# Block 3's state projection in a mixed S5 and SwiGLU layer: the shared term is added by accumulating DMAs instead of VectorE

## The chip, the cores and the metric

The kernel runs on one core of one Trainium2 chip. The metric is the device time of one execution in microseconds (us), the median over runs. Lines (L792) are those of the kernel before, and engines go by the names of the profile: PE is TensorE's matmul, PEld its weight load, DVE is VectorE, ACT is ScalarE, POOL is GpSimd, SP is SyncE.

## The reference

For one sequence of 2048 tokens with 512 features, the layer norm of x feeds two branches, and their sum is added to x. One is a diagonal state-space recurrence with 512 complex states, the other a SwiGLU of width 1792. All inputs and the output are bf16.

```python
xn = layernorm(x)
# branch A: state space
Lam_bar = exp(dt * Lam)                         # 512 complex numbers
Bu = einsum("bld,pd->blp", xn, B_bar)           # the state projection
h[t] = Lam_bar * h[t - 1] + Bu[t]
yA = 2 * real(einsum("blp,dp->bld", h, C)) + xn * Dskip
# branch B: SwiGLU
yB = (silu(xn @ w1) * (xn @ w3)) @ w2
return x + yA + yB
```

## The kernel before

**Blocks and pairs.** The tokens are cut into 4 blocks of 512 (`b` = 0 to 3), each of 4 chunks of 128. For each block there is a layer norm, the state projection, the recurrence, and the gates of the SwiGLU. Both branches' outputs are one product at the end: the tile `act` holds, for every chunk, gates and states in fp16, and it is multiplied by w2 and C together. This is done for two chunks at a time, which the code calls a pair: `pairs[n]` is block n // 2, chunks 2 (n % 2) and the next, n = 0 to 7.

**Seven products instead of eight.** The output of a pair (`y_fast`) is a 2 by 2 block product that is done with seven block products by sums and differences of the operands (Strassen's scheme in Winograd's form). `row_sums` makes the sums of the `act` side, and `product1` to `product7` are the seven, 11 matmuls each, in an order such as 1, 4, 2, 6, 5, 7, 3. One sum, s4, overwrites the operand a12 as soon as product 2 has used it. In pairs 2 to 5 this is an accumulating DMA from GpSimd's queue (L1093), and product 3 reads it as its weights. In pairs 4 and 5 product 3 is put off into the next pair (`LATER`).

**The state projection of blocks 2 and 3** (`bu_fast(b, hf)`, for each half `hf` of the states) uses the same scheme: products `one` to `seven`, four matmuls each. Of the PSUM tiles, `e` gets product five, and ScalarE copies it to SBUF as `s5`, the shared term, in f32. Two quarters of the result u are the finished PSUM tile evicted by ScalarE (`copy`). The other two are a PSUM tile plus `s5`, and VectorE adds and evicts them (`add`, L792) as bf16. In block 3 these steps are spread over the output products of pairs 2 (first half of the states) and 3 (second half), one step after each of their first five products:

```python
        return deque(((one, five), (two, six), (seven,), (three,), (four,)))
```

**The recurrence** (`ssm_tasks`) takes u through pre_a (L484) and pre_b (L488), two multiplications by a table of cosines and sines; pre_c, which adds the two, on VectorE or as an accumulating DMA (L495); four scans (L505); post_a and post_b (L513, L519), which turn back and write the states into `act`; and post_c, the sum of these two, for block 2 as an accumulating DMA (L527). In block 3 these tasks lie behind block 2's.

**What sets the order.** The order of the instructions on each engine is that of the program, which a planner (`Filler`, `bg`) writes. It keeps a queue of VectorE's background tasks (steps of the recurrence, sums, tables) with an estimated cost for each, and two clocks: `pe`, which `bg.tensor(us)` advances for each product, and `dve`, which every task and every `bg.own(us)` (VectorE work that is tied to a product) advances. `bg.fill()` emits tasks from the queue's head while they fit under `pe` plus a lead of 1.7 us:

```python
    def own(self, us, after=0.1):
        self.dve = max(self.dve, self.pe + after) + us
...
        limit = self.pe + (self.lead if lead is None else lead)
        while self.tasks and self.dve + 0.5 * self.tasks[0][0] <= limit:
```

A task that is a DMA costs 0. GpSimd's queue takes its DMAs in the order of the program, and each waits there for its own inputs.

**After pair 3** come the gates of block 3 (`glu_last`, L848, L869, L879), where VectorE does block 3's pre-steps in between, and then pairs 4 to 7.

Of the kernel before, what the change touches and what calls it, by code (L numbers as in the profile page):

```python
# [11 lines left out]
ALU = mybir.AluOpType  # L12
ACT = mybir.ActivationFunctionType

FP32 = DT.float32
BF16 = DT.bfloat16
FP16 = DT.float16
P = 128
# [45 lines left out]
def kernel(  # L64
# [17 lines left out]
    nc = tc.nc  # L82
# [4 lines left out]
    TBLK = CPB * P  # L87
# [29 lines left out]
    glup = ctx.enter_context(tc.tile_pool(name="glup", bufs=3))  # L117
# [29 lines left out]
    tabe = const.tile([P, NPT, 3, TBLK], BF16, name="tabe")  # L147
# [163 lines left out]
    gp = nc.gpsimd  # L311
# [28 lines left out]
    def sin_step(until=None):  # L340
        while sins and (until is None or until not in sins_done):
            key, fn = sins.popleft()
            fn()
            sins_done.add(key)
            if until is None:
                break
# [73 lines left out]
    def k_state(pt, ri=0):  # L420
        return (NFH if pt < NPH else NK + NFH - 2 * NPH) + 2 * pt + ri
# [13 lines left out]
    def act_state(b, hf):  # L435
        k = k_state(2 * hf)
        return act(b)[:, :, k:k + 4, :]

    def by_state(v):
        return v.rearrange("p c (j r) t -> p j r c t", r=2)  # L440

    u_blk = {}
# [19 lines left out]
    def ssm_tasks(b, posts_last=False, between=(), middle=(), late=()):  # L462
        FULL = [P, 2, 2, TBLK]

        def by_chunk(v):
            return v.rearrange("p j r (c t) -> p j r c t", t=P)

        def half(hf):
            psl = slice(2 * hf, 2 * hf + 2)
            st = {}  # L470

            def pre_a():
                if b == 0:
                    sin_step((2 * hf + 1, 1))
                    nc.vector.tensor_scalar(out=tabe[:, psl, 2, :], in0=tabe[:, psl, 1, :], scalar1=-1.0,
                                            scalar2=None, op0=ALU.mult)
                st["g"] = u_blk[b, hf]
                if (b, hf) == (3, 0):
                    st["p"] = up.tile(FULL, BF16, name="u")
                elif b == NBLK - 1:  # L480
                    st["p"] = xtp.tile([P, NDT, TBLK], BF16, name="xnT").rearrange("p (j r) t -> p j r t", r=2)
                else:
                    st["p"] = ssmw.tile(FULL, BF16, name="p")
                nc.vector.tensor_tensor(out=st["p"][:, :, ::-1, :], in0=st["g"], in1=tabe[:, psl, 2:0:-1, :],  # L484
                                        op=ALU.mult)

            def pre_b():
                nc.vector.tensor_tensor(out=st["g"], in0=st["g"], in1=tabe[:, psl, 0:1, :].to_broadcast(FULL),  # L488
                                        op=ALU.mult)

            def pre_c():
                if b == 0 or (b, hf) == (2, 0):
                    nc.vector.tensor_tensor(out=st["g"], in0=st["g"], in1=st["p"], op=ALU.add)
                else:
                    gp.dma_start(out=st["g"], in_=st["p"], accum_op=ALU.add)  # L495

            def scan(j, ri):
                pt = 2 * hf + j
                init = 0.0
                if b in (1, 2):  # L500
                    init = ends[:, hf, 2 * j + ri:2 * j + ri + 1]
                elif b > 2:
                    init = act_blk[b - 1][:, CPB - 1, k_state(pt, ri), P - 1:P]
                v = st["g"][:, j, ri, :]
                nc.vector.tensor_tensor_scan(out=v, data0=rho[:, pt:pt + 1].to_broadcast([P, TBLK]), data1=v,  # L505
                                             initial=init, op0=ALU.mult, op1=ALU.add)

            def post_a(csl=slice(0, CPB)):
                if "p16" not in st:
                    st["p16"] = ssmw.tile(FULL, BF16, name="p").bitcast(FP16).rearrange(  # L510
                        "p j r (c t) -> p (j r c t)", t=P).rearrange("p (c k t) -> p c k t", c=CPB, t=P)
                tsl = slice(csl.start * P, csl.stop * P)
                nc.vector.tensor_tensor(out=by_state(st["p16"][:, csl]), in0=by_chunk(st["g"][:, :, ::-1, tsl]),  # L513
                                        in1=by_chunk(tabe[:, psl, 2:0:-1, tsl]), op=ALU.mult)

            def post_b(csl=slice(0, CPB)):
                tsl = slice(csl.start * P, csl.stop * P)
                n = csl.stop - csl.start
                nc.vector.tensor_tensor(out=by_state(act_state(b, hf)[:, csl]), in0=by_chunk(st["g"][:, :, :, tsl]),  # L519
                                        in1=by_chunk(tabe[:, psl, 0:1, tsl]).to_broadcast([P, 2, 2, n, P]), op=ALU.mult)  # L520

            def post_c(csl=slice(0, CPB)):
                a, p16 = act_state(b, hf)[:, csl], st["p16"][:, csl]
                if b == NBLK - 1 and (hf == 1 or csl.start > 0):
                    nc.vector.tensor_tensor(out=a, in0=a, in1=p16, op=ALU.add)
                else:
                    gp.dma_start(out=a, in_=p16, accum_op=ALU.add)  # L527

            if (b, hf) == (1, 1):
                pre_c.ready = lambda: ("squares", 2, CPB - 1) in sins_done  # L530
            pre_a.ready = lambda: (b, hf) in u_blk
            scans = [lambda j=j, ri=ri: scan(j, ri) for j in range(2) for ri in range(2)]
            return (pre_a, pre_b, pre_c), scans, (post_a, post_b, post_c)

        (pre0, scans0, post0), (pre1, scans1, post1) = (half(hf) for hf in range(NPT // 2))

        transfers = (post0[2],) + (() if b == NBLK - 1 else (post1[2],)) + ((pre1[2],) if b > 0 else ()) + ((pre0[2],) if b in (1, 3) else ())

        def add(*fns):
            for fn in fns:  # L540
                bg.add(0.0 if fn in transfers else 1.2 if fn in scans0 or fn in scans1 else 1.16, fn,
                       ("scan", b) if fn in scans0 else ("post", b) if fn in post0 else ("ssm", b))

        if b == 0:
            add(*pre0, *scans0, *post0, *pre1, *scans1, *post1)
            return
        add(*pre0)
        for t in middle:
            bg.add(*t)
        if b != 2:  # L550
            add(*pre1)
        for t in between:
            bg.add(*t)
        if b == 2:
            for t in late:
                bg.add(*t)
            add(*pre1)
        add(*scans0)
        if b != 2:
            for t in late:  # L560
                bg.add(*t)
        if posts_last:
            add(*scans1)
            return lambda: add(*post0, *post1)
        if b < NBLK - 1:
            add(*post0, *scans1, *post1)
            return

        def by_tokens(fns, h):
            part = slice(h * CPB // 2, (h + 1) * CPB // 2)  # L570
            return [(0.0 if fn is post0[2] and h == 0 else 0.6, lambda fn=fn: fn(part), ("ssm", b)) for fn in fns]

        for t in by_tokens(post0, 0):
            bg.add(*t)
        add(*scans1)
        for t in by_tokens(post1, 0):
            bg.add(*t)
        return by_tokens(post0, 1) + by_tokens(post1, 1)
# [163 lines left out]
    def bu_columns(b):  # L742
        if b == 3:
            return ups["t"]
        return act(2)[:, :, k_gate(10):k_gate(10) + 4, :].rearrange("p c (k a) t -> p c k (a t)", k=2)
# [14 lines left out]
    def bu_fast(b, hf):  # L760
        a11, a12, a22 = bu_quarter(hf, 0, 0), bu_quarter(hf, 1, 0), bu_quarter(hf, 1, 1)
        s1, s2, s3, s4 = bu_rows(hf)
        t = bu_columns(b)
        t1, t2, t3, t4 = (t[i] if b == 3 else t[:, i] for i in range(4))
        b11, b12, b21, b22 = quarters(b)
        if (b, hf) == (3, 1):
            u = x_blk[3].rearrange("p (j r) t -> p j r t", r=2)
        else:
            u = up.tile([P, 2, 2, TBLK], BF16, name="u")
        s5 = glup.tile([P, 2, TBLK], BF16, name="g16").bitcast(FP32).rearrange("p a t -> p (a t)")  # L770
        if (b, hf) != (3, 1):
            f, z = (ps_bu.tile([P, TBLK], FP32, name="bu_ps") for _ in range(2))
            e, g = (ps_y.tile([P, TBLK], FP32, name="y_ps") for _ in range(2))
        else:
            f, z, e, g = (ps_gu.tile([P, TBLK], FP32, name="gu_ps") for _ in range(4))
# [8 lines left out]
        def copy(out, x):  # L784
            nc.scalar.activation(out=out, in_=x, func=ACT.Copy)

        def parts(ps):
            return ps.rearrange("p (h t) -> p h t", h=2)

        def add(out, ps):  # L790
            bg.own(0.7)
            nc.vector.tensor_tensor(out=out, in0=parts(ps), in1=parts(s5), op=ALU.add)  # L792

# [21 lines left out]
        def three():  # L815
            product(e, s4, b22)
            add(u[:, 0, :, TH:TBLK], e)
# [465 lines left out]
```

## Time and profile before

| what | value |
|---|---|
| time, median of 3 runs (lowest to highest) | 201.09 us (201.04 to 201.39) |
| span of the profiled execution, first to last instruction | 199.5 us |
| median less that span | 1.59 us |
| mean granted TensorE clock | 0.999 |
| TensorE busy | 195.6 us (98%) |
| VectorE busy | 181.8 us (91%) |
| ScalarE busy | 135.0 us (68%) |
| GpSimd busy | 51.5 us (26%) |
| L792 on VectorE, PSUM plus shared term, 128x512 | 8 of them, 0.66 to 0.69 us; 4 in block 3 |
| L785 on ScalarE, PSUM to SBUF, 128x512 to bf16 | 8 of them, 0.59 to 0.61 us |
| L1093, the DMA that makes s4, 352 KB | 3.8 us from issue to landing |
| L527, the DMA that adds the two post products, 512 KB | 5.4 to 9.1 us for the whole blocks, 4.3 us for half a block |

The profile is of one execution. Its time is the span, and what the metric adds around it is taken to be the 1.59 us between the span and the median. Busy shares are averages over stages with different limits. The chain of waits, followed back from the last instruction, tells what set the end. A landing is counted from the start of the instruction that issues the DMA.

### The profile page before, as it was taken

How to read it: one execution, taken by the hardware profiler on the slowest of the kernel's cores; microseconds unless marked ns; L12 is line 12 of the kernel's file. 1: busy time of each engine (PE TensorE's matmuls, PEld its weight loads, DVE VectorE, ACT ScalarE, POOL GpSimd, SP SyncE). 2: the span in 40 equal slices, each digit the busy share in tenths (PEclk: the TensorE clock that was granted, in tenths of full speed). 3: DMA queues.
4: the chain of work that ended last, by engine and by line, in shares of the span. 5: the costliest groups of instructions: out<-in, count | busy, mean ns of one | idle time of the engine just before them, and what ended most of it. 6: DMA issues, size and time to landing. Idle time of an engine off the chain costs nothing.

```text
span 199.5 us, 3700 instructions
## 1 busy us (share of the span) xinstructions
PE 195.6 (98%) x1401; PEld 130.7 (65%) x1401; DVE 181.8 (91%) x254; ACT 135.0 (68%) x281; POOL 51.5 (26%) x75
## 2 busy tenths in 40 slices
PE   8999999999999999999999999999999999999994
PEld 2774444444444488866555468888566678888893
DVE  3689699999999999989999997999999999999972
ACT  4699897699999996968998684362588783111220
POOL 7180289700411134041202305040021303310000
PEclk9999999999999999999999999999999999999999
DMA  4999996991497054730997455838137732941111
GB/s 138 326 277 200 302 186 124 343 273 23 69 181 141 0 105 82 135 105 0 156 148 119 89 92 98 172 83 132 53 59 129 149 56 52 174 92 36 53 44 40
DMA packets 32258, 25.12 MB, mean 126 GB/s; under 512 B 16240, under 2 KB 29936, under 8 KB 32240
## 3 DMA queue, kind: packets, MB, share of 16 engines
q0 software_dynamic: 6128, 11.38, 33.5%
q1 hardware_dynamic: 25536, 13.21, 26.8%
q10 hardware_dynamic: 576, 0.30, 0.5%
q8 instruction: 11, 0.18, 0.4%
q14 instruction: 7, 0.06, 0.1%
HBM read 7.74 MB, written 2.10 MB: 49 GB/s over the span
## 4 chain that ended last, share of the span: by engine, by line
PE 95%; DMA 2%; SPq 1%; issue 0%; DVE 0%
PE gu_ps L587 34%; PE gu_ps L1054 17%; PE y_ps L1054 10%; PE gu_ps L848 7%; PE bu_ps L1054 7%; PE bu_ps L454 3%; PE y_ps L454 3%; PE y_ps L869 3%; PE y_ps L780 3%; DMA w_sb<-in_B_w_dram 2%; PE gu_ps L619 2%; PE gu_ps L780 2%; PE bu_ps L869 1%; PE bu_ps L780 1%; PE bu_ps L619 1%; SPq L166 0%
## 5 line engine op out<-in xcount | busy, mean ns | idle before, releaser
L587 PE MATMUL gu_ps<-xnT,w_sb 128*128 128x512 bf16 x312 | 69.6, 379 | 0.0
L587 PEld LDWEIGHTS <-w_sb 128*128 128x128 bf16 x312 | 30.5, 98 | 34.2
L1054 PEld LDWEIGHTS <-act 128*128 128x128 f16 x462 | 43.5, 98 | 5.4
L596 ACT ACTIVATE g<-gu_ps 128x512 bf16<-128x512 f32 x41 | 24.8, 606 | 6.0 <-PE gu_ps L587 3.6
L597 ACT ACTIVATE u<-gu_ps 128x512 bf16<-128x512 f32 x41 | 24.8, 606 | 4.5 <-PE gu_ps L587 3.7
L505 DVE TENSOR_TENSOR_SCAN u<-rho,ends,u 128x512 bf16<-128x512 f32 x16 | 20.0, 1270 | 0.0
L527 POOL DMA_DIRECT2D act<-p x7 | 9.2, 1320 | 34.0 <-DVE act L519 22.1
L1054 PE MATMUL gu_ps<-w_sb,act 128*128 128x256 bf16 (+3 forms) x126 | 16.0, 267 | 0.0
L848 PE MATMUL gu_ps<-xnT,w_sb 128*128 128x512 bf16 x64 | 15.9, 379 | 0.0
L604 DVE TENSOR_TENSOR act<-g,u 128x1024 f16<-128x1024 bf16 x21 | 14.2, 679 | 0.4 <-ACT u L597 0.4
L860 ACT ACTIVATE g<-gu_ps 128x512 bf16<-128x512 f32 x14 | 8.4, 599 | 5.4 <-PE gu_ps L848 5.0
L454 PEld LDWEIGHTS <-bt 128*128 128x128 bf16 x64 | 6.3, 98 | 7.5
L1077 ACT ACTIVATE x_blk<-gu_ps 128x256 f32<-128x256 f32 (+1 forms) x9 | 3.3, 368 | 10.6 <-PE gu_ps L1054 10.6
L1054 PE MATMUL bu_ps<-w_sb,act 128*128 128x256 bf16 (+3 forms) x84 | 10.4, 264 | 0.0
L1054 PE MATMUL gu_ps<-ct,act 128*128 128x256 f16 (+1 forms) x72 | 10.4, 267 | 0.0
L848 PEld LDWEIGHTS <-w_sb 128*128 128x128 bf16 x64 | 6.3, 98 | 4.8
L505 DVE TENSOR_TENSOR_SCAN u<-rho,u 128x512 bf16<-128x512 f32 x8 | 9.2, 1206 | 0.0
L1054 PEld LDWEIGHTS <-x_blk 128*128 128x128 f16 x88 | 8.6, 98 | 1.0
L1054 PEld LDWEIGHTS <-tw 128*128 128x128 f16 x88 | 8.6, 98 | 1.0
L513 DVE TENSOR_TENSOR p<-u,tabe 128x2048 f16<-128x2048 bf16 (+1 forms) x8 | 8.7, 1085 | 0.1
L519 DVE TENSOR_TENSOR act<-u,tabe 128x2048 f16<-128x2048 bf16 (+1 forms) x8 | 8.7, 1083 | 0.0
L488 DVE TENSOR_TENSOR u<-u,tabe 128x2048 bf16<-128x2048 bf16 x7 | 8.5, 1219 | 0.1
(203 smaller groups left out, 392.5 us busy)
## 6 DMA issues: line engine op xcount, KB each, us to landing
act<-p POOLq DMA_DIRECT2D x6, 512.0 KB, 6.1
xn<-x_blk POOLq DMA_DIRECT2D x4, 512.0 KB, 5.5
out_dram<-xn SPq DMA_DIRECT2D x15, 128.0 KB, 1.7
w_sb<-in_B_w_dram SPq DMA_DIRECT2D x1, 1792.0 KB, 8.2
act<-act POOLq DMA_DIRECT2D x5, 352.0 KB, 4.6
w_sb<-in_B_w_dram SPq DMA_DIRECT2D x2, 768.0 KB, 6.4
u<-p POOLq DMA_DIRECT2D x3, 512.0 KB, 5.1
w_sb<-in_B_w_dram SPq DMA_DIRECT2D x4, 256.0 KB, 4.9
```

Of the source, the lines that this page charges most:

```text
L454: nc.tensor.matmul(out=ps, lhsT=bt[:, ri, dt, pt * P:(pt + 1) * P], rhs=xnT_blk[b][:, dt, :], start=(dt == 0), stop=(dt == NDT - 1))
L505: nc.vector.tensor_tensor_scan(out=v, data0=rho[:, pt:pt + 1].to_broadcast([P, TBLK]), data1=v, initial=init, op0=ALU.mult, op1=ALU.add)
L513: nc.vector.tensor_tensor(out=by_state(st["p16"][:, csl]), in0=by_chunk(st["g"][:, :, ::-1, tsl]), in1=by_chunk(tabe[:, psl, 2:0:-1, tsl]) ...
L519: nc.vector.tensor_tensor(out=by_state(act_state(b, hf)[:, csl]), in0=by_chunk(st["g"][:, :, :, tsl]), in1=by_chunk(tabe[:, psl, 0:1, tsl] ...
L527: gp.dma_start(out=a, in_=p16, accum_op=ALU.add)
L587: nc.tensor.matmul(out=ps[:, tsl], lhsT=w[:, dt, f * P:(f + 1) * P], rhs=xnT[:, dt, tsl], start=(dt == 0), stop=(dt == NDT - 1))
L596: nc.scalar.activation(out=g16[:, f % 2, :], in_=g_ps, func=ACT.Silu)
L597: nc.scalar.activation(out=u16[:, f % 2, :], in_=u_ps, func=ACT.Copy)
L604: nc.vector.tensor_tensor(out=act_gates(b, f - 1), in0=split(g16), in1=split(u16), op=ALU.mult)
L780: nc.tensor.matmul(out=out[:, h * TH:(h + 1) * TH], lhsT=left[:, h, k, :], rhs=right[:, k, :], start=(start and h == 0 and k == 0), stop=( ...
L848: nc.tensor.matmul(out=ps, lhsT=w[:, dt, f * P:(f + 1) * P], rhs=xnT[:, dt, :], start=(dt == 0), stop=(dt == NDT - 1))
L1054: nc.tensor.matmul(out=out, lhsT=left[:, k, :], rhs=right[k][:, cols], start=(start and k == 0), stop=(k == NK - 1), skip_group_check=True)
```

## The change

In block 3 alone (`by_dma`), u and the shared term `s5` are fp16. `s5` is now half of the tile that it filled as f32. The two quarters of u that need the shared term are evicted by ScalarE without it (`copy`), and then a DMA from GpSimd's queue adds `s5` to each in SBUF. There are four of these in all, two for each half of the states. VectorE's add goes, and with it the planner's `bg.own(0.7)`. Pre_a and pre_b read u as fp16 (`st["v"]`) and write bf16; everything behind them works on the bf16 view of the same memory (`st["g"]`), as before.

```diff
@@ ssm_tasks, pre_a and pre_b @@
-                st["g"] = u_blk[b, hf]
+                st["v"] = u_blk[b, hf]
+                st["g"] = st["v"].bitcast(BF16) if b in (3,) else st["v"]
...
-                nc.vector.tensor_tensor(out=st["p"][:, :, ::-1, :], in0=st["g"], in1=tabe[:, psl, 2:0:-1, :],
+                nc.vector.tensor_tensor(out=st["p"][:, :, ::-1, :], in0=st["v"], in1=tabe[:, psl, 2:0:-1, :],
                                         op=ALU.mult)
...
-                nc.vector.tensor_tensor(out=st["g"], in0=st["g"], in1=tabe[:, psl, 0:1, :].to_broadcast(FULL),
+                nc.vector.tensor_tensor(out=st["g"], in0=st["v"], in1=tabe[:, psl, 0:1, :].to_broadcast(FULL),
                                         op=ALU.mult)
@@ bu_fast @@
-        s5 = glup.tile([P, 2, TBLK], BF16, name="g16").bitcast(FP32).rearrange("p a t -> p (a t)")
+        by_dma = b in (3,)
+        if by_dma:
+            u = u.bitcast(FP16)
+            s5 = glup.tile([P, 2, TBLK], BF16, name="g16").bitcast(FP16)[:, 0, :]
+        else:
+            s5 = glup.tile([P, 2, TBLK], BF16, name="g16").bitcast(FP32).rearrange("p a t -> p (a t)")
...
         def add(out, ps):
+            if by_dma:
+                copy(out, parts(ps))
+                gp.dma_start(out=out, in_=parts(s5), accum_op=ALU.add)
+                return
             bg.own(0.7)
             nc.vector.tensor_tensor(out=out, in0=parts(ps), in1=parts(s5), op=ALU.add)
```

## The prediction

> **What bounds the kernel now.** I read the page first, for the engines and the chain that ended last.
>
> ```profile
> span 199.5 us, 3700 instructions
> PE 195.6 (98%) x1401; PEld 130.7 (65%) x1401; DVE 181.8 (91%) x254; ACT 135.0 (68%) x281; POOL 51.5 (26%) x75
> PE 95%; DMA 2%; SPq 1%; issue 0%; DVE 0%
> ```
>
> TensorE carries 95% of the chain; VectorE, which the change relieves, carries none. Next the chain in order of time, to see whether TensorE ever waits where the change works (pairs 2 and 3, 117 to 140 us). The columns are start, length, line.
>
> ```profile
> 136.01 1.20 PE bu_ps L1054 x11
> 137.21 0.44 PE gu_ps L780 x4
> 137.65 1.20 PE y_ps L1054 x11
> 138.84 1.20 PE bu_ps L1054 x11
> 140.05 3.45 PE gu_ps L848 x16
> ```
>
> Each start plus its length is the next start, and so it goes from 7.16 to 196.79 us without a hole over 0.01. So time can be lost here but not won: what VectorE saves buys nothing that TensorE waits for. The question is whether the change makes TensorE wait. The piece at 138.84 is product 3 of pair 3, whose weights come out of an accumulating DMA (line 1093). Its weight load, from the timeline of PEld:
>
> ```profile
> 138.57 1.19 PEld L1054 LDWEIGHTS <-act 128*128 128x128 f16 x11
> ```
>
> So that DMA must have landed by 138.57. The timelines of VectorE and GpSimd around it (start, length, line):
>
> ```profile
> 128.62 0.43 DVE L1065 TENSOR_TENSOR xn<-gu_ps,q 128x256 bf16<-128x256 f32 x1
> 128.96 1.27 DVE L505 TENSOR_TENSOR_SCAN u<-rho,ends,u 128x512 bf16<-128x512 f32 x1
> 130.27 1.23 DVE L513 TENSOR_TENSOR p<-u,tabe 128x2048 f16<-128x2048 bf16 x1
> 131.41 1.22 DVE L519 TENSOR_TENSOR act<-u,tabe 128x2048 f16<-128x2048 bf16 x1
> 132.55 0.42 DVE L1065 TENSOR_TENSOR xn<-bu_ps,xn 128x256 bf16<-128x256 f32 x1
> ...
> 104.78 1.27 POOL L527 DMA_DIRECT2D act<-p  x1 [8.05 <-DVE act L519]
> ...
> 132.16 0.86 POOL L1093 DMA_DIRECT2D act<-tw  x1 [8.85 <-PE bu_ps L1054]
> 132.93 1.41 POOL L527 DMA_DIRECT2D act<-p  x1
> ```
>
> And the DMA view of 130 to 142 us (40 slices of 0.3 us, then size and time from issue to landing):
>
> ```profile
> GB/s 331 96 0 0 0 0 55 0 0 0 0 28 216 207 188 207 197 160 41 174 171 177 171 171 174 177 171 177 133 10 0 0 0 0 0 140 294 27 331 82
> act<-p POOLq DMA_DIRECT2D x1, 512.0 KB, 6.3
> act<-tw POOLq DMA_DIRECT2D x1, 352.0 KB, 3.8
> ```
>
> GpSimd's queue serves one transfer after the other: bytes from 133.3, a dip at 135.4 where line 1093's end, then line 527's until 139. Line 1093 now goes first and lands at 132.16 + 3.8 = 135.96, 2.6 us before it is needed.
>
> **What goes away.** Four VectorE adds (line 792): 0.69, 0.66, 0.67 and 0.67 us, some 0.58 to 0.61 each from start to start, and a wait of 0.71 before the first. About 3.1 us of VectorE's time; on TensorE's path 0. Their planner entries go too: four bg.own(0.7).
>
> **What is added on ScalarE.** Four copies from PSUM, fp16 out. Nearest rows: the same shape to bf16, 0.59 to 0.61 (line 785); an fp16 output with a scale, 0.71 (line 395). I take 0.60, four times, 2.4 us. They fall into idle time:
>
> ```profile
> 122.94 0.58 ACT L785 ACTIVATE bu_ps<-y_ps 128x512 f32<-128x512 f32 x1
> 125.78 0.38 ACT L1077 ACTIVATE x_blk<-gu_ps 128x256 f32<-128x256 f32 x1 [2.26 <-PE gu_ps L1054]
> ```
>
> The same gap of 2.26 us stands before 137.24 in pair 3. The banks that they read come free at about 124.0 and 125.2 instead of 124.25 and 126.35, so nobody on TensorE waits longer. Were the gap gone, the copy at 125.78 would slip by 0.6, and its reader at 127.86 has more than that. Cost 0, with 0 to 0.6 as bounds. The shared term's copy changes type only (0.59 to 0.61): 0.
>
> **What is added on GpSimd's queue.** Four transfers of 128 KB (256 pieces of 512 B). Issue 0.86 to 1.28 us each (the rows of 128 and of 512 pieces). Time in the queue each: from 352 KB in 2.0 us scaled, 0.7, to half of line 527's 3.3, 1.65; I take 1.2, pieces being nearer to line 527's, and keep both ends. In pair 2 they stand behind line 495's transfer (121.77 + 7.4 = 129.2) and end by 129.2 + 2 x 1.65 = 132.5 at the latest. In pair 3 they stand behind line 1093. Their reader is pre_a (line 484) at the block's pre-steps; below.
>
> **VectorE's multiplies of fp16 by bf16.** Lines 484 and 488 get one fp16 input. The row for a mixed pair (line 834, fp16 minus bf16, 1536 wide) took 0.949 against 0.947 and 0.957 unmixed. So 0; the other bound is the f32 rate of line 792, 4 x 0.6 = 2.4 instead of 1.22, four times, as a rival.
>
> **What moves.** This is where I see the cost. With the four own(0.7) gone, the planner's tally for VectorE is lower and each fill takes tasks earlier. I went through its arithmetic from pair 2 on with the costs in the code. After product 1 of pair 3 the planner's TensorE clock is at 116.40 and the limit at 118.10. Before, the tally of 116.85 lets one task through there (post_a of block 2's first half, 1.16); post_b follows two fills later, and post_c, the DMA of line 527, only after product 2 has queued line 1093. After, two entries of 0.7 are missing since pair 2, so the last fill of that pair has let post_a out already and the tally stands at 115.65 + 1.16 = 116.81: post_b goes (117.97), then post_c with its cost of 0 (117.97 is under 118.10); the next scan does not (117.97 + 0.6). So line 527 is queued ahead of line 1093.
>
> On the clock of the trace: VectorE reaches the add at 128.62 as before (TensorE gates it), the last scan now stands before it, so post_a starts at 128.96 and post_b at 130.10 (1.14 apart, as above). Line 527 starts 1.51 after post_b's start (103.27 to 104.78; three other times 1.51 or 1.52): 131.61. Alone in its queue it landed after 5.4 us (issued at 104.78) and 6.0 (at 146.06): 137.0 to 137.6. A transfer of 352 KB right behind another landed 1.94, 2.02 and 2.14 us after it (issues at 121.23, 113.05, 157.21, each from its own landing time): so line 1093 lands at 138.95 to 139.75. I take 5.4, the quiet case, since nothing else moves then, and 2.02: 139.03. Its own issue is no limit: GpSimd is free at 131.61 + 1.28 = 132.9, and + 3.8 gives 136.7. From a landing to the weight load that waited for it passed 0.04 us (7.11 to 7.15, line 619). The weight load then starts at 139.07 instead of 138.57: TensorE waits 0.5, with 0.4 to 1.2 as bounds. Behind it on TensorE stands all that remains, and no hole takes the loss back.
>
> By the Trainium skill ("DMA: Bandwidth & Descriptors", "Anatomy of one DMA — SWDGE (gpsimd) path") a DMA of this path takes about 2.0 us plus its bytes at 436 GB/s; that would be 3.2 us for line 527, line 1093 would land near 135.7, and the sum would be 0. The trace says 5.4 to 6.0 for these 1 KB pieces, so I go by the trace.
>
> The rest that moves is covered. Block 2's second post_b and post_c come at 137.80 to 139.0 instead of 144.29 to 146.06; then VectorE waits for product 7 of pair 3 (138.84) either way and both orders are level at 140.4. Pre_a of block 3's first half moves from 146.70 to 143.5, its data landed by 132.5; the second half's from 151.23 to 146.7, its data at the latest at 139.75 + 2 x 1.65 = 143.1. Were that cover of 3.6 gone, the adds of line 879 would slip with it. Of VectorE's reads that give TensorE its banks back, line 879's come out within 0.15 us of before, and the latest, product 6 of pair 3, at 136.33 instead of 135.83: with its 0.41 it ends 0.7 ahead of product 7's first matmul (137.48). In pair 4 the DMA of line 1007 gets ahead of line 1093, but product 3 of pairs 4 and 5 is put off by a pair, 5 us and more.
>
> **Sum.** 0 + 0 + 0 + 0.5: span 199.5 to 200.0. The median of the runs, 201.09, has 1.59 around that span; 201.09 + 0.5 = 201.6, 0.25% up. A change under 0.2% (0.40 us) can hardly be told from none.
>
> **Rivals.** First, not slower: line 1093 still lands by about 138.9, so that TensorE waits under 0.4 or not at all. For it: my landing of 139.03 is only 0.1 over that point, so 0.15 us off line 527's 5.4 decides. Against: none of the rows gives an earlier landing than 138.95. Time 201.1 to 201.45; chance 0.27.
>
> The Trainium skill's fit ("DMA: Bandwidth & Descriptors", named above), taken at its word, ends here, at 201.1.
>
> Second, a longer wait: GpSimd's descriptor work for line 527 now runs beside a scan (131.24 to 132.5) and may be held for up to its 1.27 us. For it: line 495 took 1.54 at 121.77 with scans running, 0.88 at 151.26. Against: that was the third issue in a row, and line 527 at 132.93 under a scan took 1.41. Then 0.5 plus 0.6 to 1.3: 202.2 to 202.9, chance 0.10.
>
> The Trainium skill ("SBUF — State Buffer", "Who interferes with whom") says that a VectorE instruction with two SBUF inputs keeps GpSimd from reading; this rival is what that would do.
>
> Third, the mixed multiplies run at the f32 rate: (2.4 - 1.22) x 4 = 4.7 us more on VectorE from 143 on, less the 2.4 that the adds' spacing frees: 2.3, 203.4. The mixed row speaks against it; chance 0.04.
>
> Fourth, faster: it would need a hole in TensorE's chain, and there is none; only a shift of the whole run by 0.5 would show it, 200.6. Chance 0.04.
>
> **Numbers.** Forecast, a wait of 0.4 to 1.2: 0.55, 201.5 to 202.3. Slower 0.55 + 0.10 + 0.04 = 0.69, same 0.27, faster 0.04. The range takes in the first rival and the forecast (0.82): 200.9, for the spread of the runs, to 202.4.
>
> **What would show it.** Right: line 527 on GpSimd at about 131.6 and line 1093 after it; the 352 KB landing after 6 us, not 3.8; TensorE idle for about 0.5 before product 3 of pair 3, released by that DMA; no other new hole; line 792 left to block 2 alone. Wrong: line 1093 ahead of line 527 as now, or a chain without a hole (then nothing is lost), or TensorE waiting after 143 us for VectorE (then a multiply or a late landing costs, not this DMA).

## The result, and the profile after

The changed kernel takes 201.69 us (median of 10 runs, 201.49 to 202.5) against 201.24 (10 runs, 200.95 to 201.7). The ratio is 1.0029, 95% interval 1.0019 to 1.0040: slower by 0.4 to 0.8 us.

The page of the changed kernel, its engines and the chain that ended last:

```profile
span 199.8 us, 3699 instructions
PE 194.9 (98%) x1388; PEld 130.7 (65%) x1401; DVE 179.6 (90%) x250; ACT 137.2 (69%) x285; POOL 56.7 (28%) x79
PE 91%; DMA 5%; SPq 1%; issue 1%; POOL 0%; DVE 0%
```

VectorE lost 2.2 us of work, ScalarE got 2.2, GpSimd 5.2. The new thing is in the last line: DMA's share of the chain went from 2% to 5%. The chain in order of time (start, length, line) tells where:

```profile
130.32 1.22 PE bu_ps L1064 x11
131.53 0.50 POOL act L528
132.03 0.24 issue
132.28 6.64 DMA act<-tw
138.91 0.05 issue
138.96 1.38 PE bu_ps L1064 x11
```

Lines have moved: 1064, 1103 and 528 are 1054, 1093 and 527 of before. Before, TensorE's pieces followed each other here. Now the chain leaves TensorE at product 2 of pair 3, goes through GpSimd and one transfer of 6.64 us, and comes back at product 3. (The chain puts line 528's start, at 131.52, down to product 2, which runs until 131.54. What line 528 adds to is written by post_b, which ends at 130.97; it is line 1103 that needs the end of product 2.) The waits of TensorE name that transfer, and the timeline of PEld shows the weight load that waited for it:

```profile
PE bu_ps L1064 <- DMA act<-tw: 0.5, 1, 0.5
```

```profile
138.96 1.10 PEld L1064 LDWEIGHTS <-act 128*128 128x128 f16 x11 [0.73 <-DMA act<-tw]
```

VectorE and GpSimd ahead of it:

```profile
128.28 0.42 DVE L1075 TENSOR_TENSOR xn<-gu_ps,q 128x256 bf16<-128x256 f32 x1 [0.44 <-PE gu_ps L1064]
128.62 1.22 DVE L514 TENSOR_TENSOR p<-u,tabe 128x2048 f16<-128x2048 bf16 x1
129.75 1.22 DVE L520 TENSOR_TENSOR act<-u,tabe 128x2048 f16<-128x2048 bf16 x1
130.89 1.28 DVE L506 TENSOR_TENSOR_SCAN u<-rho,ends,u 128x512 bf16<-128x512 f32 x1
...
131.52 1.28 POOL L528 DMA_DIRECT2D act<-p  x1 [5.11 <-PE bu_ps L1064]
132.28 1.44 POOL L1103 DMA_DIRECT2D act<-tw  x1
135.44 2.42 POOL L799 DMA_DIRECT2D x_blk<-g  x2 [1.73 <-ACT x_blk L791]
```

Post_a and post_b (514, 520) follow the add directly, with the scan now behind them, and line 528 goes to GpSimd 0.76 us before line 1103. The transfers' view of 130 to 142 us (slices of 0.3 us; below it, from narrower windows, issue to landing):

```profile
GB/s 210 331 304 126 14 79 7 0 0 0 0 96 174 174 174 174 171 171 160 167 177 203 216 197 178 207 197 114 84 143 147 142 143 142 181 260 147 171 184 171
...
act<-p POOLq DMA_DIRECT2D x1, 512.0 KB, 5.5
act<-tw POOLq DMA_DIRECT2D x1, 352.0 KB, 6.6
```

Both kernels have the same first bytes at 133.3, but the 174 GB/s that then flow belong to line 528. Line 1103's 352 KB follow at 136.3 and land at 138.91, where they landed at 135.96 before.

One number has to be read with care. The spans differ by 0.3 us only, less than the wait. The run with the changed kernel happened to reach pair 2 earlier. The stretch from the first product of pair 2 to the first of pair 4 leaves that out; its two ends in the chain of the changed kernel are

```profile
116.78 1.20 PE gu_ps L1064 x11
...
163.39 7.21 PE gu_ps L1064 x66
```

and of before

```profile
117.12 1.20 PE gu_ps L1054 x11
...
163.10 7.21 PE gu_ps L1054 x66
```

So 163.39 - 116.78 = 46.61 us against 163.10 - 117.12 = 45.98: 0.63 us are lost in it. Behind the stretch both kernels need the same 36.4 us (199.8 - 163.39, 199.5 - 163.10). The 0.34 that the changed kernel is ahead at pair 2 stand there as early as 36 us (post_b of block 0's first half starts at 35.69 instead of 36.04), long before anything that the change touches, and over the kernels below pair 2 begins anywhere from 116.47 to 117.33.

### The profile page after: what moved, and what is told of

Its sections match the earlier page's. It is cut to its first block, busy times and chain, and to the rows that moved or that the text cites. A ratio compares the mean times of both kernels' runs of the same rounds, so it can differ in the third digit from the quotient of the medians.

```text
span 199.8 us, 3699 instructions
## 1 busy us (share of the span) xinstructions
PE 194.9 (98%) x1388; PEld 130.7 (65%) x1401; DVE 179.6 (90%) x250; ACT 137.2 (69%) x285; POOL 56.7 (28%) x79
## 4 chain that ended last, share of the span: by engine, by line
PE 91%; DMA 5%; SPq 1%; issue 1%; POOL 0%; DVE 0%
PE gu_ps L588 33%; PE gu_ps L1064 17%; PE y_ps L1064 8%; PE gu_ps L858 7%; PE bu_ps L1064 6%; PE bu_ps L454 3%; PE y_ps L454 3%; DMA act<-tw 3%; PE y_ps L879 3%; PE y_ps L786 3%; DMA w_sb<-in_B_w_dram 2%; PE gu_ps L620 2%; PE bu_ps L879 1%; PE bu_ps L786 1%; PE bu_ps L620 1%
## 5 line engine op out<-in xcount | busy, mean ns | idle before, releaser
L588 PE MATMUL gu_ps<-xnT,w_sb 128*128 128x512 bf16 x304 | 68.9, 379 | 0.4
L858 PE MATMUL gu_ps<-xnT,w_sb 128*128 128x512 bf16 x61 | 15.6, 379 | 0.1
L1017 POOL DMA_DIRECT2D act<-act x5 | 4.6, 922 | 15.9 <-DVE tw L1010 12.5
```

What stands on the lines that cost most here:

```text
L588: nc.tensor.matmul(out=ps[:, tsl], lhsT=w[:, dt, f * P:(f + 1) * P], rhs=xnT[:, dt, tsl], start=(dt == 0), stop=(dt == NDT - 1))
L858: nc.tensor.matmul(out=ps, lhsT=w[:, dt, f * P:(f + 1) * P], rhs=xnT[:, dt, :], start=(dt == 0), stop=(dt == NDT - 1))
```

## The experiments

The theory under test: the planner's tally without the four entries of 0.7 lets line 527's transfer into GpSimd's queue ahead of line 1093's, and product 3 of pair 3 waits for its place in that queue. The main rival: the four adding DMAs, or the copies on ScalarE, cost something themselves. The runs of before beside the first four kernels had a median of 200.88 us, beside the last two 201.0. "Stretch" is the one above. Line numbers differ by a few between the versions; on GpSimd in the rows below, `act<-tw` is the DMA that makes pair 3's s4, `act<-p` that of line 527.

**The change with the planner's entries kept.**

```diff
         def add(out, ps):
             if by_dma:
+                bg.own(0.7)
                 copy(out, parts(ps))
                 gp.dma_start(out=out, in_=parts(s5), accum_op=ALU.add)
                 return
```

> The changed kernel whole, with fp16 copies and the four adding DMAs, but the planner's bg.own(0.7) stays in add, so that the order of all other work is that of before. Theory (line 527's transfer ahead of line 1093's on GpSimd's queue makes product 3 of pair 3 wait): line 1093's transfer is queued first again and lands after 3.8 us, TensorE has no hole at 139, the time is that of before, 201.2 (ratio 0.999 to 1.001). Rival A (the four adding DMAs or ScalarE's four copies cost, by traffic or by holding GpSimd): the changed kernel's time stays, ratio 1.003. Rival B (the whole run is shifted by something at its start, not by product 3): 1.003 too, with the hole gone from the trace.

Measured: ratio 1.0009 (0.9996 to 1.0022), stretch 162.76 - 116.79 = 45.97. GpSimd's timeline, then the weight load of product 3:

```profile
131.83 0.88 POOL L1104 DMA_DIRECT2D act<-tw  x1 [5.41 <-PE bu_ps L1065]
132.59 1.44 POOL L528 DMA_DIRECT2D act<-p  x1
...
138.24 1.19 PEld L1065 LDWEIGHTS <-act 128*128 128x128 f16 x11
```

The order is that of before, the transfer lands after 3.9 us, and the load starts without a wait. All four adding DMAs and all four copies are in this kernel, so they cost nothing that can be measured. That VectorE is relieved of its adds gains nothing either.

**The change without the adding DMAs.**

```diff
             if by_dma:
                 copy(out, parts(ps))
-                gp.dma_start(out=out, in_=parts(s5), accum_op=ALU.add)
                 return
```

> The changed kernel without its four adding DMAs: the two quarters are copied by ScalarE and the shared term is left out of them. No bg.own(0.7), so the order is the changed kernel's. Theory: line 527 is still ahead of line 1093, its landing stays at 6.4 to 6.8 us, the weight load of product 3 waits 0.6 to 0.8, ratio 1.002 to 1.004 as the change. Rival A (the added DMAs cost): no hole, ratio 0.999 to 1.001.

Measured: ratio 1.0025 (1.0011 to 1.0039), stretch 163.01 - 116.47 = 46.54, the landing after 6.6 us. The weight load:

```profile
138.58 1.10 PEld L1063 LDWEIGHTS <-act 128*128 128x128 f16 x11 [0.66 <-DMA act<-tw]
```

With no adding DMA in the program the wait is there almost whole, 0.66 of 0.73. These two runs take the rival away from both sides.

**The tally alone, in the kernel before.**

```diff
         def add(out, ps):
-            bg.own(0.7)
+            if b != 3:
+                bg.own(0.7)
             nc.vector.tensor_tensor(out=out, in0=parts(ps), in1=parts(s5), op=ALU.add)
```

> The kernel before, with VectorE's adds from PSUM in f32 and no adding DMA, and only the planner's bg.own(0.7) left out for block 3. Theory: the order of tasks is the changed kernel's, but VectorE still does the adds, so post_b starts at about 130.7 instead of 130.1, line 527's DMA goes at 132.3 to 132.5, line 1093's lands 7.4 us later at 139.7 to 139.9, and the weight load waits 1.1 to 1.4 on that; a read of product 6 on VectorE may add up to 0.5 that mostly falls into the same wait. Ratio 1.005 to 1.008. Rival A: nothing that it blames is in this kernel, so 0.999 to 1.001.

Measured: ratio 1.0051 (1.0033 to 1.0069), stretch 164.05 - 116.92 = 47.13, so 1.15 lost. VectorE's post_b, GpSimd, and TensorE's waits:

```profile
130.49 1.22 DVE L519 TENSOR_TENSOR act<-u,tabe 128x2048 f16<-128x2048 bf16 x1
...
132.25 1.29 POOL L527 DMA_DIRECT2D act<-p  x1 [9.15 <-PE gu_ps L780]
133.01 1.45 POOL L1094 DMA_DIRECT2D act<-tw  x1
...
PE bu_ps L1055 <- DMA act<-tw: 0.5, 1, 0.5
PE y_ps L1055 <- DVE q L1066: 0.3, 1, 0.3
```

No instruction of the change is in this kernel; the planner's bookkeeping alone makes it lose more in the stretch than the whole change does, 1.15 against 0.63 (the intervals of the two ratios overlap). VectorE still does the adds, so post_b is later by the 0.6 us that were worked out (130.49 against 129.75, and this run is 0.14 behind the changed kernel's at pair 2), and so is everything behind it in the queue. The second wait is the read of product 6 on VectorE, which now comes too late for product 7. The landing came 7.3 us after the start of line 527's DMA, near the 7.4 expected, but the load of product 3 waited 0.82 for it and not 1.1 to 1.4: the loads of product 7, ahead of it, had already stood still for 0.45. Here, with the wrong order, VectorE's relief is worth 1.15 - 0.63 = 0.5 us; with the right order it was worth nothing.

**The change with s4 of pair 3 on VectorE.**

```diff
-            if n in (2, 3, 4, 5):
+            if n in (2, 4, 5):
                 gp.dma_start(out=v["s4"], in_=v["s2"], accum_op=ALU.add)
```

> The changed kernel, but s4 of pair 3 is made by VectorE (0.88 us, with the planner's entry of 0.85 that pairs 0, 1, 6 and 7 have) instead of the DMA of line 1093, so that product 3 of pair 3 needs nothing from GpSimd's queue; line 527's transfer stays where the change put it. Theory: no hole at product 3, ratio 0.999 to 1.001. Rival A: the added DMAs are all there, ratio 1.003.

Measured: ratio 1.0006 (0.9993 to 1.0019), stretch 162.86 - 116.89 = 45.97. The chain has no hole at product 3:

```profile
137.41 1.20 PE y_ps L1064 x11
138.61 1.20 PE bu_ps L1064 x11
```

Line 528 still goes early (131.63); what mattered was only who stands behind it.

**One more transfer ahead of s4.** `extra[0]` is the shared term's tile, its second half set to zero.

```diff
+            if n == 3:
+                gp.dma_start(out=extra[0][:, 1, :], in_=extra[0][:, 0, :], accum_op=ALU.add)
             if n in (2, 3, 4, 5):
                 gp.dma_start(out=v["s4"], in_=v["s2"], accum_op=ALU.add)
```

> The changed kernel with one more adding DMA between line 527's and line 1093's in pair 3: 128 KB in 128 pieces of 1 KB, from the shared term's tile into its unused half, which nothing reads (and a memset of that half on GpSimd, at pair 2). Theory: a place in the queue is what is paid for, so line 1093 lands later by this transfer's time in the queue, a quarter of line 527's 3.3 us, 0.8, and product 3 with it: the stretch from pair 2's product 1 to pair 4's (45.98 us before, 46.61 changed) gets 47.2 to 47.6, ratio to before 1.006 to 1.008. Rival (the wait at product 3 is set by GpSimd's or VectorE's work and not by the transfers ahead): 46.6 to 46.8 as in the changed kernel, ratio 1.003 to 1.004.

Measured: ratio 1.0080 (1.0061 to 1.0100), stretch 164.55 - 116.75 = 47.80.

```profile
131.49 1.28 POOL L529 DMA_DIRECT2D act<-p  x1 [5.10 <-PE bu_ps L1069]
132.24 1.44 POOL L1108 DMA_DIRECT2D g<-g  x1
132.79 1.78 POOL L1110 DMA_DIRECT2D act<-tw  x1
...
140.12 0.88 PEld L1069 LDWEIGHTS <-act 128*128 128x128 f16 x9 [1.92 <-DMA act<-tw]
```

GpSimd issues s4's DMA only 0.51 later than in the changed kernel, but it lands 1.16 later, and product 3 loses 1.19 more. So it is the transfers that are waited for, and not GpSimd's instructions. The size was missed: 0.6 to 1.0 was expected. The extra transfer landed 0.75 after line 529's (132.24 + 5.6 against 131.49 + 5.6), as worked out. S4's own landed 2.2 after that one, where it landed 1.9 after line 528's in the changed kernel; why is open.

**The change with line 527 held until s4 is queued.**

```diff
+            if (b, hf) == (2, 0):
+                post_c.ready = lambda: 3 in queued
...
                 gp.dma_start(out=v["s4"], in_=v["s2"], accum_op=ALU.add)
+                queued.add(n)
```

> The changed kernel, with block 2's first post_c (line 527) held back by the planner until pair 3's s4 (line 1093) is queued; the tasks behind it wait for it, and nothing else is edited. Theory: line 1093's transfer lands after 3.8 to 3.9 us, no hole at product 3, stretch from pair 2's product 1 to pair 4's 45.9 to 46.0, ratio to before 0.999 to 1.001. Rival (some other effect of the lower tally costs): stretch 46.3 to 46.6, ratio 1.002 to 1.003.

Measured: stretch 163.31 - 117.33 = 45.98, as before to 0.01. The order and the weight load:

```profile
132.37 0.88 POOL L1106 DMA_DIRECT2D act<-tw  x1 [5.41 <-PE bu_ps L1067]
132.92 1.66 POOL L529 DMA_DIRECT2D act<-p  x1
...
138.78 1.19 PEld L1067 LDWEIGHTS <-act 128*128 128x128 f16 x11
```

The lower tally stays, everything else still moves up, and the loss is gone. The ratio is 1.0014 (1.0002 to 1.0026), a little above what was expected. In its profile the extra 0.2 us lie ahead of pair 2, where nothing differs in the code; whether that is chance was not settled. None of these versions beats the kernel before, and with TensorE's chain whole in it none could here.

## Why the prediction was right

**The sum.** 201.6 was forecast from 201.09, a loss of 0.5. The stretch lost 0.63, and the medians differ by 0.45. The 0.63 lies in the 0.4 to 1.2 that were given for the wait. That the 0.45 of the medians comes so near 0.5 is no finer proof, with an interval of 0.4 to 0.8 around it.

**TensorE's chain has no hole.** Right, and the reason why nothing could be won: the two kernels that put the order right again have stretches of 45.97 and 45.98, against 45.98 before, and VectorE's 2.2 us fewer are worth nothing there.

**The order.** The planner's arithmetic gave the queue as it is in the trace: line 528, then 1103, then the adding DMAs of pair 3.

**The times.** Taking off the 0.34 to 0.35 that the changed kernel's run is ahead:

| step | forecast | measured |
|---|---|---|
| post_b starts | 130.10 - 0.35 = 129.75 | 129.75 |
| line 527's DMA starts, after that | 1.51 | 1.77 |
| it lands, after its start | 5.4 | 5.5 |
| line 1093's DMA lands, after that | 2.02 | 1.9 |
| weight load starts, after that | 0.04 | 0.05 |
| weight load late by | 0.50 | 0.73 |

The one term that was clearly off is the start of line 527's DMA, by 0.26; 0.1 more in its landing and 0.1 less behind it cancel. Of the rows before, four had 1.51 or 1.52, and one, the issue at 146.06, had 144.29 + 1.77. I took the four, and the prediction doesn't mention the fifth. The changed kernel's is of that other kind. In both of these the timeline names something other than post_b as waited for (VectorE's line 948 at 146.06, TensorE at 131.52), where the second one of the changed kernel, at 138.91, names post_b and starts 1.52 after it. Of the 0.73, TensorE's matmuls lost 0.63, since before a load started 0.11 ahead of its matmul.

**What was put at nothing.** The new copies of pair 2 took 0.59 and 0.60 and stood in ScalarE's gap; the multiplies with an fp16 input were no slower than before:

```profile
123.10 0.59 ACT L791 ACTIVATE u<-y_ps 128x512 f16<-128x512 f32 x1
124.30 0.60 ACT L791 ACTIVATE u<-y_ps 128x512 f16<-128x512 f32 x1 [0.61 <-PE y_ps L786]
...
143.78 1.22 DVE L485 TENSOR_TENSOR u<-u,tabe 128x2048 bf16<-128x2048 f16 x1
```

The adding DMAs landed after 6.0 and 4.4 us (medians of the two in each pair); their readers came at 143.78 and 147.11 and did not wait.

**The rivals.** That s4 would still come nearly in time, with a wait under 0.4, fell: the load waited 0.73. By the Trainium skill's fit ("DMA: Bandwidth & Descriptors", "Anatomy of one DMA — SWDGE (gpsimd) path") line 527's 512 KB would take an estimated 3.2 us; the trace says 5.5 for them alone, and the measurement decides. That a scan would hold GpSimd's descriptor work fell as well: line 528 took 1.28 with the scan of 130.89 running, where up to 1.27 more was feared. (The 1.27 at 104.78 before is no undisturbed row: a multiplication of VectorE, line 484 at 104.74, ran beside it.) The slow multiplies are refuted by the row above, and nothing got faster: no version has a shorter stretch than before by more than 0.01.

## What to carry to other kernels

Where a planner writes the order, the cost that it books for an instruction is part of the program: removing the instruction removes the booking, and tasks booked at nothing, such as DMAs, can then slip ahead of one that the bound engine waits for. Before an engine is relieved, look whether the chain that sets the end ever waits for it; if it never does, ask only what will be reordered. In a queue that serves one transfer after the other, the slack of a late reader has to hold the whole transfer that gets ahead of its own.

## What the runs showed of the hardware

An accumulating DMA in GpSimd's queue had to wait for the transfer ahead of it, and not only for that one's issue. With line 527's 512 KB in front, s4's 352 KB landed 6.6 us after their issue instead of 3.8. With 128 KB more in between they landed 1.16 later still, though issued only 0.51 later.

In all eight kernels line 527's DMA mostly started 0.3 us after post_b's end (for whole blocks 1.51 to 1.53 after its start). In nine cases it started 0.54 to 0.56 after the end (1.76 to 1.78 after the start), and there the timeline names another instruction than post_b. In each of the nine GpSimd's queue shows a wait instruction of its own ahead of the DMA, which ends 0.04 to 0.05 after post_b, with the DMA 0.5 behind it. In the others no wait instruction ends there. The changed kernel's first:

```profile
L528 POOLq EVENT_SEMAPHORE  x1: 17/17/17, 131.0 to 131.0; - x1
L528 POOL DMA_DIRECT2D act<-p x1: 1280/1280/1280, 131.5 to 131.5; - x1
```

Whether it is this extra wait instruction that costs the 0.25 was not tried.
